# A long convolution and a cosine-gated layer: the sine two chunks behind, and every other chunk's fraction without GpSimd

## The chip, the cores and the metric

The kernel runs on one core of a Trainium2 chip. The core has a matrix engine (TensorE, "PE" in the profile, with its weight loads as "PEld"), three engines for elementwise work (VectorE "DVE", ScalarE "ACT", GpSimd "POOL") and queues that issue DMA transfers (here all from SyncE, "SP"). Each engine executes its own instructions in program order and waits on semaphores for the others. The metric is the time of one execution in device microseconds; the time before is the median of three runs, 4257.37 us.

## The reference

`x` and `v` are 4 x 12480 x 128, the layer is 128 to 2048 to 128:

```python
h_filt = (np.maximum(pos_emb @ w1, 0.0) @ w2) * np.exp(-0.01 * pos)[:, None]
u = x * v
y = irfft(rfft(u, n=2*S) * rfft(h_filt, n=2*S)[None])[:, :S]   # per batch and channel
z = (x * y).reshape(B * S, D)                                  # 49920 x 128
h = z @ w_in
g = h * np.cos(h)
out = g @ w_out
```

All data are float32. The change is in the line with the cosine.

## The kernel before

**The convolution.** For each of the four batch entries the long convolution is done as a transform in two matmul stages, a product with the filter's transform, and two stages back. Its work is cut into units, stage after stage: `u` (30 units: `x*v`, sums and differences; L330 and L336), `f1` (64 units: matmuls L343, evictions L349 on ScalarE, L350 and L351 on VectorE), `f2` (48 units: matmuls L357, four products L367 and L368 on VectorE, two sums L369 on GpSimd), `i1` (64 units: matmuls L386, L394 on ScalarE, two L396 on VectorE) and `i2` (30 units: matmuls L404, L412 on VectorE). The units of f1 to i2 take a PSUM bank `cv` from a pool of two, and a unit's evictions are issued with the following unit.

**The layer.** The convolution of entry 0 is done alone at the start. Then the layer runs over 104 blocks of 480 tokens, and each block over 16 chunks of 128 of the 2048 hidden columns. One pass of the loop, a *step*, issues for chunk i:

- `moe_up`: the matmul `ph` (L569) into a PSUM bank of a pool of four; `a = ph/(2 pi) + 1/4` on ScalarE (L572); `k`, the nearest whole number to `a`, on VectorE (L575, adding and subtracting 12582912); the fraction `f = a - k` on GpSimd (L578)
- `moe_act` for chunk i-1: the sine `cs` of `2 pi f` on ScalarE (L583) and the product `gt = ph * cs` on VectorE (L585), which is the last reader of the bank `ph`
- `moe_down` for chunk i-4: the matmul `acc` (L591)
- after it, convolution units of the next batch entry, as many as the step is owed: a unit of u costs 2.1 steps, f1 and i1 1.2, f2 2.3, i2 1.6

Steps are numbered within their block, 0 to 15; `ph(6)` is the matmul of chunk 6 and `gt(3)` the product of chunk 3. Once a block three more things stand in the order: after the matmul of step 3, ScalarE copies out the finished accumulator of the block before (`ot`, L596); after step 5, four transposes (L116) bring it into a bank of the same pool of four, and VectorE copies it out (`ob`, L604); after step 8, four transposes turn the next block's input in another bank of that pool, copied out by VectorE (`at`, L564). So from entry 1's convolution on there are two kinds of blocks: those with convolution work in between, and from the end of the last convolution those without, called the tail.

**What sets the order.** All instructions stand on their engines in the order in which the program issues them; nothing reorders them. A new tile of a pool takes the slot that was freed first in program order, and waits for its last reader. For the four banks of `ph` this means that a chunk mostly waits for the product of four chunks before, and for chunks that follow a transpose it is another: the built program shows, before, `ph(6)` waiting for `gt(3)`, `ph(7)` for `gt(4)`, `ph(8)` for the copy `ob`, `ph(9)` for `gt(6)`, `ph(10)` for `gt(7)`; after the change `ph(6)` for `gt(3)`, `ph(7)` for `ob`, `ph(8)` for `gt(4)`, `ph(9)` for `gt(6)`, `ph(10)` for `at`, `ph(11)` for `gt(7)`.

Of the kernel before, what the change touches and what calls it, by code (L numbers as in the profile page):

```python
# [9 lines left out]
F32 = mybir.dt.float32  # L10
U32 = mybir.dt.uint32
AF = mybir.ActivationFunctionType
ALU = mybir.AluOpType
# [3 lines left out]
P = 128  # L17
# [5 lines left out]
TWO_PI = 6.283185  # L23

ROUND = 12582912.0
# [5 lines left out]
def kernel(  # L31
# [38 lines left out]
    nc = tc.nc  # L70
# [18 lines left out]
    TOK = 4 * N2  # L89
    NT = S // TOK  # L90
    assert NT * TOK == S and TOK <= BANK
    LAG = 4
    WCOL = 256
    UA = 2

# [13 lines left out]
    cs = const.tile([N2, 3, H], F32, name="cs")  # L109
# [9 lines left out]
    def load_words(pool, words):  # L119
        raw = pool.tile([P, WCOL, 2], U32, name="raw", bufs=4)  # L120
        nc.sync.dma_start(raw[:, :, :], words)
        return raw

    def to_float32(pool, dst, raw):
        lo, hi = raw[:, :, 0], raw[:, :, 1]

        power = pool.tile([P, WCOL], U32, name="power")
        nc.vector.tensor_scalar(out=power[:, :], in0=hi, scalar1=20, scalar2=0x7FF,
# [8 lines left out]

        sig = pool.tile([P, WCOL], U32, name="sig")
        rest = pool.tile([P, WCOL], U32, name="rest")
        nc.vector.tensor_scalar(out=rest[:, :], in0=lo, scalar1=29, scalar2=0x3F800000,  # L140
# [7 lines left out]
            in1=sig[:, :].bitcast(F32), op0=ALU.mult, op1=ALU.add)  # L148
        done = pool.tile([P, WCOL], F32, name="done", bufs=2)
        nc.vector.tensor_tensor(done[:, :], sig[:, :].bitcast(F32),  # L150
# [5 lines left out]
    weights = []  # L156
    for c in range(0, DFF, WCOL):
        weights.append((wind[:, c:c + WCOL], in_words[:, c:c + WCOL, :]))
# [399 lines left out]
    def moe_turn(pool, n):  # L558
        zb = zbs.pop(n)
        pt = ps_h.tile([P, BANK], F32, name="ph")  # L560
        for m in range(TOK // N2):
            transpose(pt[:, m * N2:(m + 1) * N2], zb[:, m, :])
        at = pool.tile([D, TOK], F32, name="at")
        nc.vector.tensor_copy(out=at[:, :], in_=pt[:, 0:TOK])  # L564
        ats[n] = at

    def moe_up(pool, n, c):
        ph = ps_h.tile([P, BANK], F32, name="ph")
        nc.tensor.matmul(ph[:, 0:TOK], w_in_sb[:, c * P:(c + 1) * P], ats[n][:, :],  # L569
                         start=True, stop=True)  # L570
        a = pool.tile([P, TOK], F32, name="a", bufs=3)
        nc.scalar.activation(a[:, :], ph[:, 0:TOK], AF.Identity,  # L572
                             bias=quarter[:, 0:1], scale=INV_TWO_PI)
        k = pool.tile([P, TOK], F32, name="k")
        nc.vector.tensor_scalar(out=k[:, :], in0=a[:, :], scalar1=ROUND,  # L575
                                scalar2=ROUND, op0=ALU.add, op1=ALU.subtract)
        f = pool.tile([P, TOK], F32, name="f")
        nc.gpsimd.tensor_tensor(f[:, :], a[:, :], k[:, :], op=ALU.subtract)  # L578
        return ph, f

    def moe_act(pool, ph, f):
        cs = pool.tile([P, TOK], F32, name="cs")
        nc.scalar.activation(cs[:, :], f[:, :], AF.Sin, scale=TWO_PI)  # L583
        gt = pool.tile([P, TOK], F32, name="gt", bufs=4)
        nc.vector.tensor_tensor(gt[:, :], ph[:, 0:TOK], cs[:, :], op=ALU.mult)  # L585
        return gt

    def moe_down(n, c, gt):
        if c == 0:
            accs[n] = ps_acc.tile([P, BANK], F32, name="acc")  # L590
        nc.tensor.matmul(accs[n][:, 0:TOK], w_out_sb[:, c, :], gt[:, :],  # L591
                         start=(c == 0), stop=(c == NFC - 1))

    def moe_evict(pool, n):
        ot = pool.tile([D, TOK], F32, name="ot", bufs=1)
        nc.scalar.copy(out=ot[:, :], in_=accs.pop(n)[:, 0:TOK])  # L596
        return ot

    def moe_store(pool, n, ot):
        pt = ps_h.tile([P, BANK], F32, name="ph")  # L600
        for m in range(TOK // N2):
            transpose(pt[0:N2, m * D:(m + 1) * D], ot[:, m * N2:(m + 1) * N2])
        ob = pool.tile([N2, TOK // N2, D], F32, name="ob", bufs=1)
        nc.vector.tensor_copy(out=ob[:, :, :].rearrange("i m d -> i (m d)"),  # L604
                              in_=pt[0:N2, :])
        nc.sync.dma_start(
            out[n * TOK:(n + 1) * TOK, :].rearrange("(m p) d -> p m d", p=N2),
            ob[:, :, :])

    with tc.manual_schedule():  # L610
        make_identity(nc, ident)
        with tc.tile_pool(name="psum", bufs=8, space=PSUM) as psum, \
# [67 lines left out]
            wpool = ctx.enter_context(tc.tile_pool(name="weights", bufs=1))  # L680
            w_in_sb = wpool.tile([D, DFF], F32, name="w_in_sb")
            w_out_sb = wpool.tile([P, NFC, D], F32, name="w_out_sb")
            quarter = wpool.tile([P, 1], F32, name="quarter")
            nc.vector.memset(quarter[:, :], 0.25)
            nc.sync.dma_start(w_in_sb[:, :], wind[:, :])
            nc.sync.dma_start(w_out_sb[:, :, :], woutd[:, :, :])
            for stage in (f2_units(bank, f2_product), i1_units(bank)):
# [16 lines left out]
        mpool = ctx.enter_context(tc.tile_pool(name="moe", bufs=2))  # L704
# [18 lines left out]
        def load(n):  # L723
            while ready < n // NT:
                next(conv)
            moe_load(mpool, n)
# [5 lines left out]
        steps = [(n, c) for n in range(NALL) for c in range(NFC)]  # L732
        hidden, gates, ots = {}, {}, {}
        for i in range(len(steps) + LAG):
            if i < len(steps):
                n, c = steps[i]
                if c == 0 and n + 2 < NALL:
                    load(n + 2)
                hidden[i] = moe_up(mpool, n, c)
            if 0 <= i - 1 < len(steps):  # L740
                gates[i - 1] = moe_act(mpool, *hidden.pop(i - 1))
            if i >= LAG:
                pn, pc = steps[i - LAG]
                moe_down(pn, pc, gates.pop(i - LAG))
                if pc == NFC - 1:
                    ots[pn] = moe_evict(mpool, pn)
            if i < len(steps):
                if c == LAG + 1 and n - 1 in ots:
                    moe_store(mpool, n - 1, ots.pop(n - 1))
                if c == NFC // 2 and n + 1 < NALL:  # L750
                    moe_turn(mpool, n + 1)
            owed += share
            while owed > 0.0:
                owed -= next(conv, owed)
# [32 lines left out]
```

## Time and profile before

| | before |
|---|---|
| median of 3 runs | 4257.37 us (4257.25 to 4261.64) |
| the profiled execution | 4264.29 us |
| its span in the trace | 4262.5 us |
| busy: TensorE | 3916.4 us (92%) |
| busy: VectorE | 3047.8 us (72%) |
| busy: GpSimd | 2546.8 us (60%) |
| busy: ScalarE | 2415.2 us (57%) |
| mean clock granted to TensorE | 0.954 |

A group of instructions is read so: line, engine, operation, output and inputs by the program's names, sizes, count; then busy time and mean nanoseconds of one; then the engine's idle time just before them and what ended it. In a timeline each line gives start, duration, engine, line and operation, and in brackets the idle time before it and what ended that.

### The profile page before, as it was taken

How to read it: one execution, taken by the hardware profiler on the slowest of the kernel's cores; microseconds unless marked ns; L12 is line 12 of the kernel's file. 1: busy time of each engine (PE TensorE's matmuls, PEld its weight loads, DVE VectorE, ACT ScalarE, POOL GpSimd, SP SyncE). 2: the span in 40 equal slices, each digit the busy share in tenths (PEclk: the TensorE clock that was granted, in tenths of full speed). 3: DMA queues.
4: the chain of work that ended last, by engine and by line, in shares of the span. 5: the costliest groups of instructions: out<-in, count | busy, mean ns of one | idle time of the engine just before them, and what ended most of it. 6: DMA issues, size and time to landing. Idle time of an engine off the chain costs nothing.

```text
span 4262.5 us, 49170 instructions
## 1 busy us (share of the span) xinstructions
PE 3916.4 (92%) x13882; PEld 2244.3 (53%) x13882; DVE 3047.8 (72%) x6588; ACT 2415.2 (57%) x4484; POOL 2546.8 (60%) x2311
## 2 busy tenths in 40 slices
PE   5868778999999998998899989988999999999999
PEld 3836673554456653554466634644466644444444
DVE  8657669987778568777776588766675566666666
ACT  1343155775567445655455456644554577777777
POOL 2422347657865457568854476568754577777776
PEclk8557889999999999999999999999999999999999
DMA  3354343112211442012201531022103400000000
GB/s 86 89 167 120 96 136 106 50 52 78 82 51 42 142 142 85 15 50 81 75 12 51 177 112 42 15 73 78 52 15 107 127 19 19 19 19 19 19 19 14
DMA packets 271763, 293.63 MB, mean 69 GB/s; under 512 B 16741, under 2 KB 204101, under 8 KB 271237
## 3 DMA queue, kind: packets, MB, share of 16 engines
q1 hardware_dynamic: 271493, 290.50, 23.6%
q8 instruction: 112, 1.84, 0.2%
q14 instruction: 158, 1.29, 0.1%
HBM read 210.12 MB, written 80.31 MB: 68 GB/s over the span
## 4 chain that ended last, share of the span: by engine, by line
PE 65%; POOL 11%; DVE 10%; ACT 5%; DMA 5%; issue 3%; SPq 0%; DVEq 0%; POOLq 0%; ACTq 0%
PE ph L569 24%; PE acc L591 23%; POOL f L578 6%; POOL slots L369 5%; PE cv L404 4%; PE cv L386 4%; ACT cs L583 3%; PE cv L343 3%; PE ps L343 3%; DVE gt L585 2%; DMA w<-wd 2%; DMA hd<-h 2%; PE ph L116 2%; DVE slots L336 1%; PE ps L386 1%
## 5 line engine op out<-in xcount | busy, mean ns | idle before, releaser
L578 POOL TENSOR_TENSOR f<-a,k 128x480 f32<-128x480 f32 x1664 | 2021.9, 1218 | 1174.9 <-DVE k L575 1174.9
L569 PE MATMUL ph<-at,w_in_sb 128*128 128x480 f32 x3328 | 1647.4, 577 | 102.6 <-DVE gt L585 101.6
L591 PE MATMUL acc<-gt,w_out_sb 128*128 128x480 f32 x3328 | 1618.0, 568 | 0.5 <-DVE gt L585 0.5
L572 ACT ACTIVATE a<-ph,quarter 128x480 f32<-128x480 f32 x1664 | 1094.2, 658 | 750.7 <-PE ph L569 691.8
L585 DVE TENSOR_TENSOR gt<-ph,cs 128x480 f32<-128x480 f32 x1664 | 1091.7, 656 | 476.3 <-ACT cs L583 452.7
L583 ACT ACTIVATE cs<-f 128x480 f32<-128x480 f32 x1664 | 998.4, 600 | 690.6 <-POOL f L578 688.7
L575 DVE TENSOR_SCALAR k<-a 128x480 f32<-128x480 f32 x1664 | 778.8, 468 | 528.3 <-ACT a L572 514.4
L591 PEld LDWEIGHTS acc<-gt,w_out_sb 128*128 128x128 f32 x3328 | 633.8, 190 | 715.5 <-issue 713.5
L569 PEld LDWEIGHTS ph<-at,w_in_sb 128*128 128x128 f32 x3328 | 584.8, 191 | 575.4 <-issue 290.4
L369 POOL TENSOR_TENSOR slots<-slots,t 120x256 f32<-120x256 f32 x384 | 296.6, 795 | 228.2 <-DVE t L368 176.6
L357 PE MATMUL ps<-slots,w 124*120 124x256 f32 x384 | 165.9, 576 | 80.7 <-DVE w L250 45.6
L386 PEld LDWEIGHTS cv<-cs,slots 120*96 120x96 f32 x1536 | 180.5, 168 | 82.0 <-issue 72.1
L357 PE MATMUL cv<-slots,w 124*120 124x256 f32 x576 | 155.3, 390 | 49.7 <-PE acc L591 36.0
L404 PEld LDWEIGHTS cv<-slots,tm 96*104 96x104 f32 x1440 | 173.1, 171 | 46.7 <-issue 36.0
L386 PE MATMUL cv<-cs,slots 120*96 120x120 f32 x1536 | 191.2, 267 | 3.3 <-POOL slots L369 3.3
L404 PE MATMUL cv<-slots,tm 96*104 96x128 f32 x1440 | 178.7, 275 | 11.0 <-DMA tm<-td 7.2
L343 PEld LDWEIGHTS cv<-c,slots 104*124 104x124 f32 x768 | 130.6, 192 | 84.4 <-issue 54.8
L357 PEld LDWEIGHTS ps<-slots,w 124*120 124x120 f32 x384 | 93.0, 268 | 153.0 <-issue 70.5
L357 PEld LDWEIGHTS cv<-slots,w 124*120 124x120 f32 x576 | 98.7, 182 | 134.3 <-PE acc L591 78.0
L343 PE MATMUL cv<-c,slots 104*124 104x192 f32 x768 | 159.5, 330 | 3.2 <-POOL slots L336 2.6
L396 DVE TENSOR_TENSOR slots<-cv,other 96x240 f32<-96x240 f32 x384 | 135.9, 393 | 0.5
L330 POOL TENSOR_TENSOR xt<-xt,vt 104x512 f32<-104x512 f32 x30 | 38.3, 1276 | 137.5 <-DMA vt<-in_v_dram 127.0
(111 smaller groups left out, 2781.8 us busy)
## 6 DMA issues: line engine op xcount, KB each, us to landing
h<-hd SPq DMA_DIRECT2D x192, 240.0 KB
tm<-td SPq DMA_DIRECT2D x90, 312.0 KB
xt<-in_x_dram SPq DMA_DIRECT2D x120, 208.0 KB
vt<-in_v_dram SPq DMA_DIRECT2D x120, 208.0 KB
xs<-in_x_dram SPq DMA_DIRECT2D x120, 208.0 KB
zd<-zs SPq DMA_DIRECT2D x120, 208.0 KB
zb<-zd SPq DMA_DIRECT2D x104, 240.0 KB
out_dram<-ob SPq DMA_DIRECT2D x104, 240.0 KB
```

The source lines that it names most:

```text
L343: nc.tensor.matmul(ps[0:KE, i * 2 * N1:(i + 1) * 2 * N1], u[:, b, 0:KE, i], c1[0:u.shape[0], :, :].rearrange("p r k -> p (r k)"), start=Tr ...
L357: nc.tensor.matmul(ps[0:N2, i * 2 * D:(i + 1) * 2 * D], w[:, i, :], parts[0:KE, :, k1 + i, :, :], start=True, stop=True)
L369: nc.gpsimd.tensor_tensor(y[:, r], y[:, r], t[:, r], op=op)
L386: nc.tensor.matmul(ps[0:N1, (i * 2 + r) * N2:(i * 2 + r + 1) * N2], parts[0:N2, r, :, b, i], cs[:, r:r + 2, :].rearrange("p c a -> p (c a) ...
L404: nc.tensor.matmul(ps[0:R, i * D:(i + 1) * D], t[:, i, r, :], slots[0:N1, :, place, :], start=(r == 0), stop=(r == 1))
L569: nc.tensor.matmul(ph[:, 0:TOK], w_in_sb[:, c * P:(c + 1) * P], ats[n][:, :], start=True, stop=True)
L572: nc.scalar.activation(a[:, :], ph[:, 0:TOK], AF.Identity, bias=quarter[:, 0:1], scale=INV_TWO_PI)
L575: nc.vector.tensor_scalar(out=k[:, :], in0=a[:, :], scalar1=ROUND, scalar2=ROUND, op0=ALU.add, op1=ALU.subtract)
L578: nc.gpsimd.tensor_tensor(f[:, :], a[:, :], k[:, :], op=ALU.subtract)
L583: nc.scalar.activation(cs[:, :], f[:, :], AF.Sin, scale=TWO_PI)
L585: nc.vector.tensor_tensor(gt[:, :], ph[:, 0:TOK], cs[:, :], op=ALU.mult)
L591: nc.tensor.matmul(accs[n][:, 0:TOK], w_out_sb[:, c, :], gt[:, :], start=(c == 0), stop=(c == NFC - 1))
```

## The change

Three edits. The sine and the product are issued two chunks behind the scaling `a` instead of one. For odd chunks `k` is made on ScalarE, as `a + 12582912` by an Identity activation with a bias tile, and VectorE makes `(k - 12582912) - a`, the negated fraction, in one instruction; the sine's scale is negated to match. In odd steps these two are issued behind the sine and the product of that step; in even steps `k` and `f` stay on VectorE and GpSimd and ahead of them. The tiles `k` and `f` have three buffers instead of two.

```diff
+    SINE_LAG = 2
...
-        k = pool.tile([P, TOK], F32, name="k")
-        nc.vector.tensor_scalar(out=k[:, :], in0=a[:, :], scalar1=ROUND,
-                                scalar2=ROUND, op0=ALU.add, op1=ALU.subtract)
-        f = pool.tile([P, TOK], F32, name="f")
-        nc.gpsimd.tensor_tensor(f[:, :], a[:, :], k[:, :], op=ALU.subtract)
-        return ph, f
-
-    def moe_act(pool, ph, f):
+        return ph, a
+
+    def moe_fold(pool, a, c):
+
+        k = pool.tile([P, TOK], F32, name="k", bufs=3)
+        f = pool.tile([P, TOK], F32, name="f", bufs=3)
+        if c % 2 == 0:
+            nc.vector.tensor_scalar(out=k[:, :], in0=a[:, :], scalar1=ROUND,
+                                    scalar2=ROUND, op0=ALU.add, op1=ALU.subtract)
+            nc.gpsimd.tensor_tensor(f[:, :], a[:, :], k[:, :], op=ALU.subtract)
+            return f, TWO_PI
+        nc.scalar.activation(k[:, :], a[:, :], AF.Identity, bias=whole[:, 0:1])
+        nc.vector.scalar_tensor_tensor(out=f[:, :], in0=k[:, :], scalar=ROUND, in1=a[:, :],
+                                       op0=ALU.subtract, op1=ALU.subtract)
+        return f, -TWO_PI
+
+    def moe_act(pool, ph, f, scale):
         cs = pool.tile([P, TOK], F32, name="cs")
-        nc.scalar.activation(cs[:, :], f[:, :], AF.Sin, scale=TWO_PI)
+        nc.scalar.activation(cs[:, :], f[:, :], AF.Sin, scale=scale)
...
+            whole = wpool.tile([P, 1], F32, name="whole")
+            nc.vector.memset(whole[:, :], ROUND)
...
-                hidden[i] = moe_up(mpool, n, c)
-            if 0 <= i - 1 < len(steps):
-                gates[i - 1] = moe_act(mpool, *hidden.pop(i - 1))
+                ph, a = moe_up(mpool, n, c)
+                if c % 2 == 0:
+                    hidden[i] = (ph,) + moe_fold(mpool, a, c)
+            if 0 <= i - SINE_LAG < len(steps):
+                gates[i - SINE_LAG] = moe_act(mpool, *hidden.pop(i - SINE_LAG))
+            if i < len(steps) and c % 2 == 1:
+                hidden[i] = (ph,) + moe_fold(mpool, a, c)
```

In the changed kernel's own numbering `a` is L573, VectorE's `k` L582, GpSimd's `f` L584, ScalarE's `k` L586, VectorE's `f` L587, `cs` L593, `gt` L595, `acc` L601, `ot` L606, `ob` L614, and the lines of the convolution are one higher.

## The prediction

> **What bounds the kernel now.** I read the page's groups of costliest instructions first, for durations. The change touches these:
>
> ```profile
> L578 POOL TENSOR_TENSOR f<-a,k 128x480 f32<-128x480 f32 x1664 | 2021.9, 1218 | 1174.9 <-DVE k L575 1174.9
> L572 ACT ACTIVATE a<-ph,quarter 128x480 f32<-128x480 f32 x1664 | 1094.2, 658 | 750.7 <-PE ph L569 691.8
> L585 DVE TENSOR_TENSOR gt<-ph,cs 128x480 f32<-128x480 f32 x1664 | 1091.7, 656 | 476.3 <-ACT cs L583 452.7
> L583 ACT ACTIVATE cs<-f 128x480 f32<-128x480 f32 x1664 | 998.4, 600 | 690.6 <-POOL f L578 688.7
> L575 DVE TENSOR_SCALAR k<-a 128x480 f32<-128x480 f32 x1664 | 778.8, 468 | 528.3 <-ACT a L572 514.4
> ```
>
> Second, the timeline of the copy L564, which comes once per block of 16 chunks: its distances are block times. They fall into six stages, named after the convolution work interleaved. One block of each, as a table of busy time by stretch (stretch, length, then busy time and count of PE, PEld, DVE, ACT, POOL; clock, DMA share, GB/s), in the order u, f1, f2, i1, i2, tail:
>
> ```profile
> 1617.10:1653.80 36.70, 29.90 (x72) 12.06 (x72) 33.48 (x51) 19.07 (x33) 27.88 (x25) 1.00 0.35 106
> 1796.10:1832.20 36.10, 36.02 (x129) 21.73 (x128) 27.21 (x64) 24.15 (x47) 19.02 (x17) 1.00 0.05 15
> 1982.30:2020.50 38.20, 34.26 (x102) 17.43 (x101) 27.19 (x63) 19.14 (x33) 30.94 (x31) 1.00 0.29 80
> 2209.70:2247.80 38.10, 38.10 (x183) 23.76 (x182) 27.05 (x63) 22.52 (x47) 18.89 (x17) 1.00 0.05 14
> 2374.60:2419.00 44.40, 44.40 (x235) 30.48 (x234) 24.46 (x46) 19.55 (x33) 19.30 (x17) 1.00 0.58 177
> 3710.20:3736.80 26.60, 26.60 (x73) 12.91 (x72) 18.32 (x35) 20.41 (x34) 19.28 (x17) 1.00 0.07 18
> ```
>
> TensorE never stops in f1, i1, i2 and the tail; only u and f2 have room. In the tail four matmul records 0.40 us apart are one chunk, 1.61 us; 16 of them and two transposes (0.44, 0.41) make 26.6.
>
> Third, the timeline of f2, for the wait that costs there:
>
> ```profile
> 2008.67 2.56 POOL L578 TENSOR_TENSOR f<-a,k 128x480 f32<-128x480 f32 x2
> ...
> 2010.11 0.60 ACT L583 ACTIVATE cs<-f 128x480 f32<-128x480 f32 x1 [2.31 <-POOL f L578]
> ...
> 2010.74 0.66 DVE L585 TENSOR_TENSOR gt<-ph,cs 128x480 f32<-128x480 f32 x1 [1.73 <-ACT cs L583]
> ...
> 2011.46 1.07 PE L569 MATMUL ph<-at,w_in_sb 128*128 128x480 f32 x2 [1.11 <-DVE gt L585]
> ```
>
> A late fraction on GpSimd holds the sine, the product, the PSUM bank, and TensorE. Last, f1, where a wait is nearly one already:
>
> ```profile
> 858.01 0.66 DVE L585 TENSOR_TENSOR gt<-ph,cs 128x480 f32<-128x480 f32 x1
> ...
> 858.96 0.35 DVE L351 TENSOR_SCALAR slots<-cv 60x192 f32<-60x192 f32 x1
> ...
> 859.43 0.76 PEld L343 LDWEIGHTS cv<-c,slots 104*124 104x124 f32 x4 [0.38 <-issue]
> ```
>
> L351 frees the convolution's bank at 859.31; TensorE loads for it at 859.43.
>
> [...] f2's weight loads wait for L585, which frees one of four banks. [...] a and cs alternate here back to back (0.64 us at 2010.62, the next at 2011.27). [...] L330 (two SBUF inputs) took 0.69 us alone and 0.85 us beside GpSimd work covering all of it: slowed, not blocked.
>
> **Costs of the new instructions.** k of an odd chunk on ScalarE, SBUF to SBUF: like cs, 0.60 us (bounds: 0.545, the copy L596; 0.66, like a). f of an odd chunk on VectorE: L250, the same operation, takes 0.43 us for 208 elements; 272 more [...] give 0.71 (bounds 0.66 as a plain product, 1.2 if blocked for one GpSimd f). Removed: 832 GpSimd f's (1.22 us) and 832 VectorE k's (0.41 alone, 0.47 on average). ScalarE in the tail rises from 20.4 to 20.4 + 8 x 0.60 = 25.2 us of 26.6: it still fits, 3.12 us against TensorE's 3.22 per pair. No DMA is moved; the one memset added at the start is one small instruction (the least VectorE row here is 0.33 us). Waits are what counts. Handoffs from the timeline: ph start to a start 1.01, cs to gt 0.03, gt to the next ph 0.05.
>
> **Tail (32.3 blocks).** gt of chunk i now follows a of chunk i+2, not i+1, so its bank comes free a step later, and ph(i) has two steps of slack where it had three. The loop a, cs, gt, ph is 1.01+0.66+0.60+0.03+0.66+0.05 = 3.01 us: fits two steps (3.22). But twice a block a transpose takes one of the four banks (after steps 5 and 8), and the bank order in the built program makes ph(6) wait for gt(3) and ph(9) for gt(6), both issued one step earlier. There the loop has to fit into one step. ph(6): ScalarE is 0.40 late, since the copy ot (0.54, step 3) isn't made up at 0.1 per pair; so 0.40 + 3.01 = 3.41 after ph(5), where TensorE would be ready at 1.61+0.44 = 2.05: 1.36 lost. ph(9): a(8) waits for k(7), 0.25: 3.26 against 1.61+0.41: 1.24 lost. Remainders in later steps 0.2. Sum 2.8 x 32.3 = **+90**. Before, the same two waits had a step more and cost nothing.
>
> **f1 (14.4 blocks) and i1 (14.4).** In an odd step VectorE is in order: gt, then f, which waits for k at the end of ScalarE's a, cs, k; behind it the evictions L350 and L351, and TensorE's next convolution matmuls wait for these (two cv banks). From ph at 0: a 1.01 to 1.67, cs to 2.27, k to 2.87; gt 2.30 to 2.96, f to 3.67, evictions (0.36+0.35) to 4.38. TensorE is there at 2.25+1.61 = 3.86: it waits until 4.43, 0.57 lost. In the old order (k to 2.18, gt to 2.96, evictions to 3.67) it had 0.19 left, as the last lines above show. A unit comes every 1.2 steps, so both steps of a pair have one in 0.67 x 8 = 5.3 pairs: 3.05; ph(6) and ph(9) have longer steps to fit into here: 3.01 against 2.25+0.44 is 0.3, and 3.2 (k(7) and an eviction ahead on ScalarE) against 2.25+0.41 is 0.6: 3.9 x 14.4 = **+56**. i1 likewise: the two L396 (0.39) end at 4.45+0.05 against 2.43+1.61: 0.46 x 5.3, and 0.5 for ph(6) and ph(9) against steps of 2.43, = 3.0 x 14.4 = **+43**. i2 (9 blocks): evictions have time, only ph(6) and ph(9), in steps without a unit: 0.8, **+7**.
>
> **f2 (20.7 blocks, 38.4 us on average).** ScalarE no longer waits for a fraction made in the same step, and GpSimd has half the f's. VectorE then bounds: 16 x 0.66 (gt) + 8 x 0.41 + 8 x 0.71 + 0.65 + 0.68 (at, ob) + 7 x 4 x 0.415 (L367, L368) = 32.4. Add 1.5 for ph(6) and ph(9), where its products only partly fill the hole[...]: 35.2, a gain of 3.2: **-66**. **u (11.8 blocks, 36.6 us):** likewise 10.6+3.3+5.7+1.3 + 7.6 x (0.86+0.87) = 34.0, plus 1.5 and 1.3: 36.8, no change to count: **0**.
>
> Sum: 90+56+43+7-66+0 = **+130 us** on the profiled execution (4264.29, span 4262.5), hence about 4394; on the median of the runs, 4257.37, which is 7 lower: **4387**.
>
> **Rivals.**
> - *GpSimd blocks the new f* (0.13): in f2 and u f takes 1.2 us; f2's gain is gone (66) and u loses 2 a block (24): 4477. For it: a k took 1.06 us in u (663.93). Against: L330's 0.85.
> - *Banks don't bind* (0.08): if TensorE's slack covers ph(6) and ph(9), the tail's 90, i2's 7 and their share in f1 and i1 (13+7) fall away: +13, 4270. Against: f2's weight loads do wait for L585.
> - *Faster* (0.09): evictions wait for nothing new because f finds k done; f1 and i1 lose nothing, and f2 and u reach VectorE's sums without surcharge (-6.0 x 20.7 - 2.6 x 11.8 = -155): 90+7-155 = -58, 4199. It decides once f1 and i1 together lose under 58 instead of 99 with those gains. For it: 0.9 to 1.9 us waits on GpSimd fill u and f2. Against: the order in the odd step.
> - *The change doesn't do what it says*: excluded; GpSimd's f's halve in the built order.
>
> **How the numbers follow.** The sum has 0.68, itself 4320 to 4450 (tail 2.2 to 3.6 a block; f1 and i1 half to 1.2 of theirs; f2's gain 1.5 to 4.5); 0.02 for neither. The range takes in the bank rival's edge and the blocked f: 4275 to 4475. A change within 0.2% (8.5 us) can't be told from none here; near it lie the lower edge of the bank rival and chance crossings. Faster 0.10, same 0.04, slower 0.86.
>
> **What would show it.** Tail blocks of about 29.4 instead of 26.6, with weight loads of L570 waiting for gt (L595) over 1 us twice a block, near L614 and L565; f1 blocks near 39.5 and i1 near 40.6, with L344 and L387 waiting for VectorE's L352 and L397; f2 blocks near 35. Mean durations: k (L586) 0.60, f (L587) 0.71. Wrong would be: tail blocks under 27, an f over 1 us, f2 blocks not shorter.

## The result, and the profile after

The changed kernel takes 4302.53 us (median of four runs, 4298.19 to 4303.53) against 4259.51 us for the kernel before in the same comparison: a ratio of 1.0098, 95% interval 1.0081 to 1.0116. It is slower, as forecast, by 43 us instead of 130. The profiled execution took 4298.19 us, with a span of 4296.4 us, 33.9 more than before, at nearly the same granted clock (0.957 and 0.954).

Where the time went is read from the distances between the block copies (L564 before, L565 after). The table gives the mean length of the blocks that lie wholly within a stage, and what all blocks of the stage together gained or lost:

| stage | before, us | after, us | all blocks, us | forecast, us |
|---|---|---|---|---|
| u | 36.60 | 33.82 | -24.8 | 0 |
| f1 | 35.97 | 38.90 | +39.6 | +56 |
| f2 | 38.52 | 34.39 | -80.6 | -66 |
| i1 | 37.81 | 39.69 | +24.7 | +43 |
| i2 | 44.43 | 45.02 | +12.1 | +7 |
| tail | 26.62 | 28.57 | +60.8 | +90 |
| sum | | | +31.6 | +130 |

All signs are as forecast; for u no change was forecast. The three large losses are 57% to 71% of their forecasts, and the two stages that gain do so by more than forecast.

In the groups of costliest instructions of the kernel after, ScalarE's `k` took 0.683 us (forecast 0.60), VectorE's `f` 0.671 (forecast 0.71, an estimate: 0.43 for the 208 elements of L250, and for 272 more the 1.05 ns by which L351, 192 in 0.353, and L585, 480 in 0.656, differ, give 0.72), and the sine's idle time fell from 690.6 us to 0.3. The weight loads of `ph` are idle for 616 us in all, of which 384 us end with a `gt`; before it was 575 us and 265:

```profile
L595 DVE TENSOR_TENSOR gt<-ph,cs 128x480 f32<-128x480 f32 x1664 | 1091.0, 656 | 787.2 <-ACT cs L593 761.4
...
L593 ACT ACTIVATE cs<-f 128x480 f32<-128x480 f32 x1664 | 989.3, 595 | 0.3 <-DVE f L587 0.3
L570 PEld LDWEIGHTS ph<-at,w_in_sb 128*128 128x128 f32 x3328 | 586.1, 190 | 615.9 <-DVE gt L595 383.9
L586 ACT ACTIVATE k<-a,whole 128x480 f32<-128x480 f32 x832 | 568.7, 683 | 0.0
L587 DVE SCALAR_TENSOR_TENSOR f<-k,a 128x480 f32<-128x480 f32 x832 | 558.5, 671 | 2.3 <-issue 1.0
```

One block of each stage after, in the same columns and the same order (u, f1, f2, i1, i2, tail) as the table by stretch of before:

```profile
1612.80:1645.50 32.70, 29.08 (x72) 12.31 (x72) 29.49 (x52) 23.43 (x41) 15.67 (x17) 1.00 0.43 118
1793.80:1832.80 39.00, 37.64 (x129) 21.61 (x128) 28.96 (x64) 28.35 (x55) 9.63 (x9) 1.00 0.05 13
1975.40:2010.30 34.90, 33.50 (x100) 17.84 (x100) 29.22 (x64) 23.11 (x41) 20.14 (x23) 1.00 0.32 88
2194.40:2234.40 40.00, 39.65 (x187) 24.00 (x185) 29.00 (x64) 26.93 (x55) 9.76 (x9) 1.00 0.05 14
2364.60:2409.00 44.40, 44.40 (x234) 30.48 (x234) 26.02 (x45) 23.32 (x41) 9.67 (x9) 1.00 0.61 181
3704.50:3733.10 28.60, 27.36 (x72) 12.85 (x72) 19.64 (x35) 22.76 (x41) 9.68 (x9) 1.00 0.07 18
```

TensorE (the first busy column) is no longer full in f1 and in the tail. Its idle time there understates the loss (1.24 us in the tail block, where 1.95 are lost), because busy time is modelled; the weight loads show the waits themselves. In a tail block of the kernel before, `ph(6)` follows `ph(5)` by 2.05 us, and `ph(9)` follows `ph(8)` by 2.02; an ordinary step takes 1.61. The two lines are `ph(5)` and `ph(6)` of before:

```profile
3728.42 0.97 PE L569 MATMUL ph<-at,w_in_sb 128*128 128x480 f32 x2
...
3730.47 0.97 PE L569 MATMUL ph<-at,w_in_sb 128*128 128x480 f32 x2
```

After the change the first line below is `ph(5)`; `ph(6)` follows 2.91 us later, and `ph(9)` 2.92 us after `ph(8)`.

```profile
3724.09 0.97 PE L570 MATMUL ph<-at,w_in_sb 128*128 128x480 f32 x2
...
3726.28 0.66 DVE L595 TENSOR_TENSOR gt<-ph,cs 128x480 f32<-128x480 f32 x1 [0.48 <-ACT cs L593]
...
3727.00 1.07 PE L570 MATMUL ph<-at,w_in_sb 128*128 128x480 f32 x2 [0.48 <-DVE gt L595]
...
3730.32 0.97 PE L570 MATMUL ph<-at,w_in_sb 128*128 128x480 f32 x2
...
3733.24 1.07 PE L570 MATMUL ph<-at,w_in_sb 128*128 128x480 f32 x2 [0.73 <-DVE gt L595]
```

The timeline of an odd step of f1 shows the eviction behind the fraction: `f` stands before L351 and L352, and the convolution's matmul waits for L352.

```profile
1810.82 0.66 DVE L587 SCALAR_TENSOR_TENSOR f<-k,a 128x480 f32<-128x480 f32 x1
...
1811.79 0.35 DVE L352 TENSOR_SCALAR slots<-cv 60x192 f32<-60x192 f32 x1
...
1812.29 0.89 PE L344 MATMUL cv<-c,slots 104*124 104x192 f32 x4 [0.28 <-DVE slots L352]
```

And f2's timeline still has waits for a bank, though no longer for a late fraction:

```profile
1981.61 0.30 PEld L570 LDWEIGHTS ph<-at,w_in_sb 128*128 128x128 f32 x2 [0.84 <-DVE gt L595]
```

### The profile page after: what moved, and what is told of

Its sections match the earlier page's. It is cut to its first block, busy times and chain, and to the rows that moved or that the text cites. A ratio compares the mean times of both kernels' runs of the same rounds, so it can differ in the third digit from the quotient of the medians.

```text
span 4296.4 us, 50355 instructions
## 1 busy us (share of the span) xinstructions
PE 3930.3 (91%) x13882; PEld 2243.6 (52%) x13882; DVE 3177.8 (74%) x6589; ACT 2776.8 (65%) x5316; POOL 1510.3 (35%) x1479
## 4 chain that ended last, share of the span: by engine, by line
PE 66%; DVE 15%; ACT 10%; DMA 5%; issue 4%; POOL 0%; SPq 0%; DVEq 0%; ACTq 0%; POOLq 0%
PE ph L570 27%; PE acc L601 21%; DVE gt L595 5%; ACT a L573 4%; PE cv L387 4%; PE cv L405 4%; ACT cs L593 3%; PE ps L344 3%; PE cv L358 2%; PE cv L344 2%; DMA w<-wd 1%; DVE f L587 1%; DMA hd<-h 1%; DMA zd<-zs 1%; PE ps L387 1%
## 5 line engine op out<-in xcount | busy, mean ns | idle before, releaser
L573 ACT ACTIVATE a<-ph,quarter 128x480 f32<-128x480 f32 x1664 | 1094.5, 658 | 1113.8 <-PE ph L570 1090.3
L584 POOL TENSOR_TENSOR f<-a,k 128x480 f32<-128x480 f32 x832 | 1002.9, 1205 | 2208.2 <-DVE k L582 2208.2
L595 DVE TENSOR_TENSOR gt<-ph,cs 128x480 f32<-128x480 f32 x1664 | 1091.0, 656 | 787.2 <-ACT cs L593 761.4
L601 PE MATMUL acc<-gt,w_out_sb 128*128 128x480 f32 x3328 | 1614.2, 567 | 0.5 <-DVE gt L595 0.3
L601 PEld LDWEIGHTS acc<-gt,w_out_sb 128*128 128x128 f32 x3328 | 632.0, 190 | 712.4 <-issue 709.5
L593 ACT ACTIVATE cs<-f 128x480 f32<-128x480 f32 x1664 | 989.3, 595 | 0.3 <-DVE f L587 0.3
L586 ACT ACTIVATE k<-a,whole 128x480 f32<-128x480 f32 x832 | 568.7, 683 | 0.0
L587 DVE SCALAR_TENSOR_TENSOR f<-k,a 128x480 f32<-128x480 f32 x832 | 558.5, 671 | 2.3 <-issue 1.0
L582 DVE TENSOR_SCALAR k<-a 128x480 f32<-128x480 f32 x832 | 347.8, 418 | 116.2 <-ACT a L573 112.2
L370 POOL TENSOR_TENSOR slots<-slots,t 120x256 f32<-120x256 f32 x384 | 285.2, 765 | 262.5 <-DVE t L369 154.0
```

What stands on the lines that cost most here:

```text
L573: nc.scalar.activation(a[:, :], ph[:, 0:TOK], AF.Identity, bias=quarter[:, 0:1], scale=INV_TWO_PI)
L586: nc.scalar.activation(k[:, :], a[:, :], AF.Identity, bias=whole[:, 0:1])
L587: nc.vector.scalar_tensor_tensor(out=f[:, :], in0=k[:, :], scalar=ROUND, in1=a[:, :], op0=ALU.subtract, op1=ALU.subtract)
L593: nc.scalar.activation(cs[:, :], f[:, :], AF.Sin, scale=scale)
```

## The experiments

The theory after the comparison: the lag of two causes the bank waits (tail, i2) and the gain of f2; the *split* (odd fractions on ScalarE and VectorE) causes the loss of f1 and i1. The gain of u and the sizes were open. Block lengths in us for all runs:

| run | u | f1 | f2 | i1 | i2 | tail | time, us | ratio to before, interval |
|---|---|---|---|---|---|---|---|---|
| before | 36.60 | 35.97 | 38.52 | 37.81 | 44.43 | 26.62 | | |
| after | 33.82 | 38.90 | 34.39 | 39.69 | 45.02 | 28.57 | 4302.5 | 1.0098 (1.0081-1.0116) |
| lag_only | 37.89 | 36.25 | 34.62 | 38.25 | 45.02 | 28.57 | 4288.7 | 1.0067 (1.0052-1.0082) |
| split_only | 36.21 | 39.23 | 37.59 | 39.82 | 44.37 | 30.22 | 4427.6 | 1.0391 (1.0374-1.0409) |
| five_banks | 31.42 | 38.67 | 33.27 | 39.40 | 45.00 | 27.55 | 4207.8 | 0.9878 (0.9864-0.9893) |
| five_one_cv | 31.43 | 77.84 | 61.22 | 76.44 | 76.91 | 26.62 | 6082.4 | one run |
| f_late | 33.41 | 37.68 | 35.11 | 38.60 | 45.03 | 28.58 | 4277.1 | 1.0040 (1.0025-1.0055) |
| fold_late | 33.40 | 36.61 | 35.11 | 38.25 | 45.02 | 28.57 | 4253.8 | 0.9984 (0.9977-0.9991) |
| k_twice | 34.29 | 40.35 | 35.00 | 40.88 | 45.03 | 30.44 | 4420.8 | one run |
| fold_late_five | 31.37 | 36.06 | 33.03 | 37.82 | 44.61 | 26.97 | 4115.8 | 0.9663 (0.9649-0.9678) |
| lag_five | 36.58 | 35.67 | 33.00 | 37.82 | 44.60 | 26.97 | 4157.5 | 0.9762 (0.9746-0.9779) |
| before_five | 37.49 | 36.07 | 38.43 | 37.86 | 44.65 | 27.31 | 4302.1 | 1.0100 (1.0085-1.0115) |
| f_half_five | 29.09 | 35.67 | 32.95 | 37.82 | 44.61 | 26.97 | 4070.6 | one run |

**The lag alone, the split alone.**

```diff
 lag_only (in moe_fold, and where it is called)
-        if c % 2 == 0:
+        if True:
...   (the call for odd steps falls away)
 split_only
-    SINE_LAG = 2
+    SINE_LAG = 1
```

> The lag of two alone: every chunk's k on VectorE and f on GpSimd, as before the change, only the sine and product one chunk later. Theory A (the tail's loss is the bank waits of ph(6) and ph(9), which the lag makes; the loss in f1 and i1 is the odd step's f ahead of the evictions; the gain in f2 and u comes from the lag, which takes GpSimd out of ScalarE's wait): tail blocks 28.5 as after the change, f1 blocks near 36.3 and i1 near 38.0 (only the bank waits), f2 near 34.5, u near 34.0; together about 4230. Rival B (the loss is the k's that ScalarE does in addition, 8 x 0.68 us a block): tail, f1 and i1 blocks as before the change (26.6, 35.7, 37.7). Rival C (the gain is GpSimd's halved work): f2 and u blocks as before the change (38.4, 36.6).

> The split alone: odd chunks' k on ScalarE and f on VectorE, the sine and product one chunk behind as before the change. Theory A: tail 26.6 (no bank wait, ScalarE has room), f1 near 38 and i1 near 39 (the odd step's f is still ahead of the evictions), f2 and u between before and after the change (37, 36), since every even chunk's sine still waits for GpSimd; together about 4290. Rival B: tail 28.5. Rival C: f2 near 34.5 and u near 34 as after the change.

The tail with the lag alone is that of the whole change to a hundredth, 28.57 us, though ScalarE makes no `k` in it: the tail's loss is the lag's. So is the gain of f2 (34.62; with the split alone 37.59). The loss of f1 and i1 is the split's (39.23 and 39.82, against 36.25 and 38.25). The gain of u belongs to neither alone: the split alone takes 0.4 us off a block of u, the lag alone adds 1.3 (34.0 was expected, hence 4288.7 us instead of 4230), and both together take off 2.8.

The tail of the split alone, 30.22 us, was a surprise. Its timeline shows a closed loop through VectorE, GpSimd, ScalarE and VectorE that comes round once per pair of chunks:

```profile
3903.50 0.40 DVE L582 TENSOR_SCALAR k<-a 128x480 f32<-128x480 f32 x1
...
3904.05 1.21 POOL L584 TENSOR_TENSOR f<-a,k 128x480 f32<-128x480 f32 x1 [2.45 <-DVE k L582]
...
3905.28 0.60 ACT L593 ACTIVATE cs<-f 128x480 f32<-128x480 f32 x1 [0.51 <-POOL f L584]
...
3906.58 0.66 DVE L587 SCALAR_TENSOR_TENSOR f<-k,a 128x480 f32<-128x480 f32 x1
...
3907.15 0.40 DVE L582 TENSOR_SCALAR k<-a 128x480 f32<-128x480 f32 x1
```

From one VectorE `k` (3903.50) to the next (3907.15) are 3.65 us, where two steps of TensorE take 3.22. Eight such rounds are 29.2 us of the 30.22. With a lag of one, the even chunk's sine waits for GpSimd's fraction, the odd chunk's `k` stands behind that sine on ScalarE, the odd fraction waits for it, and the next even `k` stands behind that on VectorE. With a lag of two the sine has its fraction already. This is read from the trace; no further run tested it.

**A fifth bank.** The kernel's pools hold eight banks (four `ph`, two accumulators, two `cv`). The fifth for `ph` is taken from the accumulators, or in *five_one_cv* from `cv`.

```diff
 five_banks
-        ps_acc = ctx.enter_context(tc.tile_pool(name="ps_acc", bufs=2, space=PSUM))
-        ps_h = ctx.enter_context(tc.tile_pool(name="ps_h", bufs=4, space=PSUM))
+        ps_acc = ctx.enter_context(tc.tile_pool(name="ps_acc", bufs=1, space=PSUM))
+        ps_h = ctx.enter_context(tc.tile_pool(name="ps_h", bufs=5, space=PSUM))
 five_one_cv: ps_acc stays at 2, ps_c goes from 2 to 1
```

> The changed kernel with five PSUM banks for ph, and one for the accumulator instead of two (it is copied out a step before it is written again). Theory A: the tail's blocks go from 28.57 back to 26.6 (32 x 1.95 = 62 us), f1 and i1 lose about 0.6 and 0.3 a block less, f2 gains a little more; 4302 - 62 - 13 - 10 = about 4217. Rival B: tail blocks stay at 28.5 and the time at 4300.

> The changed kernel with five ph banks and two accumulators again, and one bank for the convolution instead of two. If the tail's rest with five banks (27.55 instead of 26.62) is the wait of the first acc for the copy ot out of the single accumulator, tail blocks are 26.6; otherwise they stay at 27.5. The convolution's stages lose by the missing bank, which is not asked here.

With five banks and both accumulators the tail is 26.62 us, the same as before: the bank waits are its whole loss. (With a single convolution bank f1 and i1 take about twice as long, in f1 also at a lower granted clock, 0.76 in one of its blocks and 0.879 over the run. This run was made for the tail, where the clock is 1.00.) With one accumulator 0.9 us of the loss remain. They lie in one step of the block, 2.54 us instead of 1.61; in it the first accumulation waits for ScalarE to copy the old result out, and 0.66 us show as TensorE's wait.

```profile
3711.43 0.54 ACT L606 COPY ot<-acc 128x480 f32<-128x480 f32 x1
...
3712.03 1.07 PE L601 MATMUL acc<-gt,w_out_sb 128*128 128x480 f32 x2 [0.66 <-ACT ot L606]
```

f2 and u gained from the fifth bank as well (1.1 and 2.4 us a block): bank waits cost there too. In i2 the fifth bank gains nothing (45.00 against 45.02), because one wait takes the place of another: in the four full i2 blocks of the first and third convolution TensorE waits 0.72 us per block for `gt` after the change, and with five banks instead 0.66 us for `ot`.

**The fraction behind the evictions.** In *f_late* only VectorE's odd `f` is issued after the convolution unit of its step; in *fold_late* ScalarE's `k` goes with it.

```diff
 fold_late
-            if i < len(steps) and c % 2 == 1:
-                hidden[i] = (ph,) + moe_fold(mpool, a, c)
...   (the loop that issues the step's convolution units)
+            if i < len(steps) and c % 2 == 1:
+                hidden[i] = (ph,) + moe_fold(mpool, a, c)
```

> The changed kernel with the odd chunk's f on VectorE issued at the end of the step, behind the convolution's evictions, and nothing else moved. Theory A: f1 blocks from 38.7 to about 36.5 and i1 from 39.7 to about 38.2 (14.4 x 2.2 + 14.4 x 1.5 = 53 us); tail and f2 within 0.3 of the changed kernel's; together about 4250. Rival B: f1 and i1 stay at 38.7 and 39.7, and the time at 4300.

> The changed kernel with both halves of the odd chunk's fraction, k on ScalarE and f on VectorE, issued at the end of the step, behind the convolution's evictions of both engines. If the rest that f_late left in f1 (37.7 against 36.25 with the lag alone) is k ahead of ScalarE's eviction L350, for which L351 waits: f1 near 36.3, i1 near 38.2, f2 near 35, tail 28.5; together 4240 to 4250. If the rest has another cause, f1 stays at 37.7 and the time near 4275.

f1 goes from 38.90 to 37.68 with `f` behind (36.5 was expected), and to 36.61 with `k` behind as well. So moving `f` back recovers 1.2 us of the 2.9, and moving `k` back as well another 1.1; what is left is close to the lag alone (36.25). In *f_late* L351 had become the one that waits, for ScalarE's L350: 1.88 us per block on average (one of these waits is the 0.29 us at 1797.55), and 0.1 in *fold_late*. `k` was not moved alone, so these are gains in this order and not two separate costs. In i1 `f` alone recovers 1.1 us, and with `k` the block is that of the lag alone (38.25).

**A second `k`.** ScalarE makes every odd `k` twice; nothing reads the copy.

```diff
         nc.scalar.activation(k[:, :], a[:, :], AF.Identity, bias=whole[:, 0:1])
+        kk = pool.tile([P, TOK], F32, name="kk")
+        nc.scalar.activation(kk[:, :], a[:, :], AF.Identity, bias=whole[:, 0:1])
```

> The changed kernel with ScalarE's k of every odd chunk made twice (the second copy is read by nobody). If a ScalarE instruction occupies its engine as long as its record lasts, a tail block has 16 x 0.66 + 16 x 0.60 + 16 x 0.68 + 0.55 = 31.6 us of ScalarE and takes at least that. If instructions that don't wait for each other start every 0.5 to 0.6 us, as the timeline after the change shows (a to cs 0.56, cs to k 0.49, k to a 0.58), it has about 26.8, and the block grows only by what the second k adds ahead of a(8): 28.6 to 29.5.

The tail rises to 30.44 us. That lies between the two expectations: less than the 31.6 that the records would need, more than the 28.6 to 29.5 that the starts gave. The timeline shows ScalarE without a pause between three instructions, and tells what its instructions really take:

```profile
3865.91 0.68 ACT L586 ACTIVATE k<-a,whole 128x480 f32<-128x480 f32 x1
...
3866.50 0.68 ACT L588 ACTIVATE kk<-a,whole 128x480 f32<-128x480 f32 x1
...
3867.08 0.64 ACT L573 ACTIVATE a<-ph,quarter 128x480 f32<-128x480 f32 x1
```

Records of 0.68 us start 0.59 and 0.58 us apart: instructions that wait for nothing overlap by about 0.1. The durations of a block add up to 16 x 0.66 + 16 x 0.595 + 16 x 0.683 + 0.55 = 31.6 us, more than the block they fit into. By starts, a pair with two `k` takes 3.25 us (0.55 + 0.49 + 0.55 + 0.49 + 0.58 + 0.59), just over TensorE's 3.22: no slack is left for `ot`, and ordinary steps become longer too (four take 6.82 us in one block instead of 6.44, and `ph(9)` comes 3.50 us after `ph(8)` instead of 2.92). The expectation by starts counted none of this. With one `k` it takes 2.66, and slack is ample.

**Late fold and five banks together.** The two edits of *fold_late* and *five_banks*.

> The same with five ph banks and one accumulator bank. If the losses are the two named (bank waits by the lag, evictions behind the odd chunk's fraction) they add up: 4208 of five_banks less the 50 to 60 of fold_late, and in the tail the copy ot is no longer behind k, so that the wait for the single accumulator falls from 0.9 to about 0.4: blocks near 27.1; together about 4140. If they overlap: no better than 4190.

At 4115.8 us, where about 4140 was expected, this beats both kernels, 3.4% below the kernel before. So the losses add up. The tail comes to 26.97 us instead of 27.55, since `ot` on ScalarE now stands ahead of that step's `k`. (*lag_five* below has no `k` on ScalarE, and the same tail.)

**What each part is worth once banks suffice.** *lag_five* is *lag_only* with five banks and one accumulator, *before_five* the kernel before with them.

> The lag of two alone, with all k on VectorE and all f on GpSimd, and five ph banks with one accumulator. It tells whether the split is worth anything once the banks suffice. If the split only costs (theory: it puts work ahead of the evictions, and its gain in u was the banks), this is at or below the version with the split's late fold and five banks: tail 26.6 to 27.0, f1 35.7, i1 37.5, f2 33, u 31.4 to 32, about 4110 us. If the split is needed in u because GpSimd's f holds VectorE's updates off there (rival), u stays at 35 to 36 and the rest is as above: about 4150 to 4170 us.

> The kernel before with five ph banks and one accumulator, no lag and no split. It tells whether the lag has any part in the gain. If five banks alone give it (rival), f2 falls from 38.5 to about 33 and u from 36.6 to about 31.4: about 4120 us. If the lag is what f2 needs (theory: there the chain of one chunk, not the banks, sets the pace, so that f2 stays above 36.5), the time is 4200 to 4270 us; the tail is 26.6 to 27.6 in both, the more if the first accumulation of a block waits for the only accumulator to be emptied.

Five banks without the lag gain nothing: f2 stays at 38.43, and one accumulator costs 0.7 us per tail block. (The time, 4302.1, lies above the 4200 to 4270 expected; u too got longer.) With the lag, f2 is at 33.0. So in f2 the lag had to come first, and the bank was the next limit. And *lag_five* and *fold_late_five* agree within 0.4 us in every stage but u, where they differ by 5.2. So the rival in the expectation of *lag_five* held: the split's whole worth is in u, 423.1 - 375.8 = 47 us over its blocks, 42 us in the time.

**Why u needs the split.** In *f_half_five* GpSimd's fraction is made for half the tokens, and the sine reads that half twice, so the right fraction of the other half is left out; VectorE's and ScalarE's lists of instructions are those of *lag_five*.

```diff
-            nc.gpsimd.tensor_tensor(f[:, :], a[:, :], k[:, :], op=ALU.subtract)
+            nc.gpsimd.tensor_tensor(f[:, 0:HALF], a[:, 0:HALF], k[:, 0:HALF], op=ALU.subtract)
...
-        nc.scalar.activation(cs[:, :], f[:, :], AF.Sin, scale=scale)
+        nc.scalar.activation(cs[:, :].rearrange("p (i j) -> p i j", i=2),
+                             f[:, 0:HALF].unsqueeze(1).to_broadcast([P, 2, HALF]),
+                             AF.Sin, scale=scale)
```

> The lag of two alone with five ph banks, and GpSimd's f made for the first 240 of the 480 tokens only; the sine reads these 240 twice, so that the other half of each chunk's gate is computed from the wrong fraction. VectorE's and ScalarE's lists of instructions stay as they are in the lag with five banks; GpSimd's f takes about half, so its total falls to what the split leaves it. Theory (in u GpSimd's fractions hold VectorE's instructions off while both run): VectorE's own durations there (0.68 and 0.60 for the units of u, 0.40 for k, 0.66 for gt) add up to 28.4 us a block, and the hold shrinks from 8.1 to 1 to 3: u 29.5 to 31.5 instead of 36.6, and the means of k and of the product x*v in u come down from 0.70 and 1.25 us. Rival (u is set by something else, such as the four bank waits or VectorE's list itself): u stays at 35.5 to 36.6 with the same means. In both, f1, f2, i1, i2 and the tail stay within 0.3 us, except that f2 may shorten by up to 2.

u falls from 36.58 to 29.09 us, a little below what the theory gave, and no other stage moves by more than 0.05. The means in u fall from 0.70 to 0.46 us for `k`, and from 1.25 to 0.85 for `x*v`. First the timeline of *lag_five* in u, then the corresponding stretch of *f_half_five*:

```profile
1585.92 1.20 POOL L584 TENSOR_TENSOR f<-a,k 128x480 f32<-128x480 f32 x1 [0.68 <-DVE k L582]
...
1586.33 1.06 DVE L582 TENSOR_SCALAR k<-a 128x480 f32<-128x480 f32 x1
...
1587.47 1.21 POOL L584 TENSOR_TENSOR f<-a,k 128x480 f32<-128x480 f32 x1 [0.34 <-DVE k L582]
...
1587.88 1.34 DVE L331 TENSOR_TENSOR xt<-xt,vt 104x512 f32<-104x512 f32 x1
```

```profile
1546.02 0.69 POOL L586 TENSOR_TENSOR f<-a,k 128x240 f32<-128x240 f32 x1 [0.68 <-DVE k L584]
...
1546.43 0.55 DVE L584 TENSOR_SCALAR k<-a 128x480 f32<-128x480 f32 x1
...
1547.06 0.70 POOL L586 TENSOR_TENSOR f<-a,k 128x240 f32<-128x240 f32 x1 [0.34 <-DVE k L584]
...
1547.47 0.84 DVE L331 TENSOR_TENSOR xt<-xt,vt 104x512 f32<-104x512 f32 x1
```

In both, VectorE's `k` starts 0.41 us after a GpSimd fraction, and so does L331. When the fraction gets 0.51 us shorter, `k` and L331 get 0.51 and 0.50 shorter. Left alone they take 0.40 and 0.68. In both kernels `k` ends 0.27 us after the fraction does, and L331 0.54 to 0.55 after it. So, by these distances, VectorE's instruction starts, stands until GpSimd's ends, and then runs on. Not every VectorE instruction is held: before the change 852 of the products `gt` started while a fraction ran, and all took 0.66 us. What makes an instruction wait was not shown. VectorE never pauses in u in either kernel (0.03 and 0.14 us of idle per block before its `k`, none before the rest), so the hold is paid in full. In f2 it is not: VectorE's mean `k` falls from 0.67 to 0.43 us, and the block stays at 33.0, because TensorE is full there (32.80 of 32.80 us in both).

## Why the prediction was right in sign and wrong in size

**The step that failed** is the pricing of an engine's time, of ScalarE first: "k of an odd chunk on ScalarE, SBUF to SBUF: like cs, 0.60 us", and from it "3.12 us against TensorE's 3.22 per pair". Durations of records were added as if one began where the other ended. By starts the pair takes 2.66 us. The lines that the prediction itself named held it (a record of 0.60 us at 2010.11, the next ScalarE start at 2010.62). Two errors partly cancel: `k` is longer than was said (0.683), but each record overlaps the next by 0.1. *k_twice* tests it: by the records its tail could not have been shorter than 31.6 us, and it was 30.44. The same addition stands in the price of f2, for VectorE.

**Tail, 60.8 instead of 90.** The mechanism held: `ph(6)` and `ph(9)` wait, and with enough banks nothing is lost. Two terms were mis-sized, both by ScalarE's price. For `ph(6)`, "ScalarE is 0.40 late" is wrong: with 0.56 us of slack per pair it has made up for `ot` by then. The loop is also 0.1 shorter, as the sine starts 0.56 us after `a`, not 0.66. 3.01 - 0.1 = 2.91, as measured; lost are 2.91 - 2.05 = 0.86, not 1.36. For `ph(9)`, "a(8) waits for k(7), 0.25" did not happen: 2.92 - 2.02 = 0.90, not 1.24. The first two matmuls after a stall took 1.07 us together instead of 0.97, twice a block, and the next step began 0.1 later: 0.86 + 0.90 + 0.2 = 1.96, which is the measured 28.57 - 26.62. The forecast had 0.2 as well, for remainders in later steps; there are none, so that agreement is luck. Some 4 us more come from counting 32.3 blocks, where there are 31.

**f1 and i1, 39.6 and 24.7 instead of 56 and 43.** The same term. With starts 0.56 and 0.49 us apart, ScalarE's `k` ends at 2.74 instead of 2.87, `gt` at 2.86, `f` at 3.53, the evictions at 4.24. TensorE waits 0.43 instead of 0.57 per crossing, or 2.3 in f1. The 0.9 for `ph(6)` and `ph(9)` in f1 was too much as well: the lag alone adds 0.28, and a fifth bank takes 0.23 off. Together that is 2.6; measured 2.9, and the rest stays open. In i1, 0.32 x 5.3 + 0.3 = 2.0; measured 1.9. What *f_late* and *fold_late* add is a second wait that the prediction did not see: it named VectorE's evictions behind `f`, and not ScalarE's eviction behind `k`, which held f1 by itself once `f` was out of the way. In one place it read its own lines too generously: L351 freed the bank 0.12 us ahead of the load, not 0.19.

**f2, -80.6 instead of -66.** The direction and the bank surcharge (1.5) held: the fifth bank took 1.1 off. The bound was misnamed. "VectorE then bounds", at 32.4, plus 1.3 for what VectorE loses beside GpSimd (0.06 per `k`, its mean of 0.47 less the 0.41 alone; 0.1 per `f`, for which nothing measured stood), should have been TensorE, 32.8 to 33.0; shorter holds on VectorE do not change that (33.00 in *lag_five*, 32.95 in *f_half_five*). The 32.4 is again a sum of records: in the f2 block of the table after, VectorE's records add up to 32.4 us, and it was busy for 29.22, since its records overlap as well. That 35.2 came near the measured 34.39 is partly luck. With the fifth bank the block is near TensorE's limit (33.27), without it at 34.39. The gain is also not the same in the three convolutions (3.2, 3.4 and 5.7 us a block); why is open.

**u, -24.8 instead of 0.** The reading "slowed, not blocked", from one L330 of 0.85 us beside GpSimd work, was wrong. The GpSimd work beside it was two instructions, and L330 overlapped the first, a fraction, by only 0.31 us:

```profile
1557.06 1.21 POOL L578 TENSOR_TENSOR f<-a,k 128x480 f32<-128x480 f32 x1 [0.34 <-DVE k L575]
...
1557.96 0.85 DVE L330 TENSOR_TENSOR xt<-xt,vt 104x512 f32<-104x512 f32 x1
```

It ended 0.54 us after the fraction, as L331 does in the last experiment. All 78 products `x*v` of the kernel before that overlap the end of a fraction by over 0.15 us end 0.55 us after it, whether they are 0.85 or 1.25 us long. So the sum for u, with 7.6 x (0.86+0.87) for its units, counted held records as VectorE's own work; the shortest records are 0.69 and 0.41. After the change the mean of the sums (L336, then L337) in u falls from 0.87 to 0.60 us and that of VectorE's `k` from 0.69 to 0.40, while `x*v` rises from 0.88 to 0.97. The rival "GpSimd blocks the new f" put the right mechanism to the wrong use: the new `f` was held at times (mean 0.83 us in u of the kernel after), but taking half of GpSimd's fractions away freed more than that.

**i2** cost 12.1 instead of 7, about 1 us a block in the first and third convolution and nothing in the two full blocks of the second; why the second differs is open.

Together: 29 us of the miss are the tail, 35 f1 and i1, 15 f2, 25 u, and i2 gives 5 back, which makes about 98 before rounding, between the forecast of +130 and the blocks' +31.6. The medians differ by 9 us more than the two profiled executions do. Two further readings of the prediction were off without effect: the one memset added is like L684, which took 0.06 us, not 0.33; and 3.2 against 2.25+0.41 is 0.5, not 0.6.

## What to carry to other kernels

Take an engine's occupancy from the distances between starts in a stretch where it never waits, not from the sum of its records (a tail block of *k_twice*: 31.6 us by ScalarE's records, 30.44 measured). Where two engines hold each other up, as VectorE and GpSimd do here (`x*v` of 0.69 us took up to 1.25 before the change, GpSimd's sum of 0.73 up to 1.19), price the records of both, and ask which of them are held: taking work off GpSimd can be worth more to VectorE than the work put on it (in u, with five banks, the split was worth 47 us over its blocks). And a longer lag between stages needs its buffers with it: here f2 gained 81 us with it and the tail lost 61, until a fifth bank was given to it.

## What the runs showed of the hardware

- ScalarE instructions that wait for nothing start 0.49 to 0.59 us apart while their records last 0.595 to 0.683; VectorE's overlap too (in *lag_five*, `gt`, 0.66 us long, is followed after 0.57).
- A VectorE instruction held by GpSimd has a long record and no idle time before it: `k` of 0.40 us showed as 1.06, L331 of 0.68 as 1.34. In three kernels it ended 0.26 to 0.27 us (`k`) or 0.54 to 0.55 us (`x*v`) after the fraction that held it. Such a wait is found in the durations and not among the waits.
- GpSimd was held in the same way: its sum (L336, 0.73 us at its shortest) took 1.17 to 1.19 in all 77 cases where it began over 0.15 us before the end of VectorE's `x*v`, and ended 0.58 to 0.60 after it.
- The first two `ph` matmuls after a stall took 1.07 us together instead of 0.97.
- A single accumulator made a tail block 0.93 us longer with `ot` behind `k` (*five_banks*), and 0.35 with `ot` ahead of it (*fold_late_five*).
